# One fused attention, routing and two-MLP kernel: first transfers in a fixed order, another order inside attention, a shorter rational function, and all weight conversions behind the last routing

## The chip, the cores and the metric

One core of a Trainium2 chip runs the whole program in one launch. The metric is device time in microseconds (us). TensorE (PE) multiplies matrices, VectorE (DVE), ScalarE (ACT) and GpSimd (POOL) work on elements, SyncE (SP) issues nearly all transfers, in order.

## What is computed

```python
# 1: causal attention with decay; B, H, S, D = 4, 8, 576, 64
cum = cumsum(log(clip(f, 1e-4, 1)), -1)
scores = q @ k.T / sqrt(D) + cum[i] - cum[j]          # j <= i
x = softmax(scores) @ v                               # to 2304 tokens x 512
# 2: eight experts, one per token
logits = x @ w_gate + modality_bias[modality_id]
e, gate = argmax(logits), softmax(logits).max()
x = gate * (relu(x @ w1[e]) @ w2[e])                  # 512 -> 1024 -> 512
# 3: a second MLP with a rational activation
h = x @ w_in                                          # 512 -> 2048
g = (a0 + a1 h + a2 h^2 + a3 h^3) / (1 + |b0 h| + |b1| h^2 + 1e-6)
out = g @ w_out
```

`w_in`, `w_out`, `a` and `b` come as 64-bit floats; the rest is 32-bit.

## The kernel before

**Attention** works on 16 pairs of heads. For a pair, `load` brings k, q and v (nine transfers), `parts` turns k and q with PE and splits them into a high and a low part (`split`: a copy on ACT, a difference on DVE), `maxes` computes the scores once in four groups M0 to M3 to get each row's maximum (a DVE reduction per block), `turned` turns the maxima and sends them by two transfers into a row of the operand `qa`, `scores` computes the scores again in S0 to S3 with that row, exponentiates (ACT) and splits (ACT, POOL), and `values` multiplies with v in chunks (V) and divides. `logits` (L0, L1) of a finished pair turns its result and adds to the routing logits. The string `ORDER` writes down in which order PE takes these steps of four different pairs in one pass of the loop: M of pair p+1, S of p, V of p-1, L of p-2, T (`parts`) of p+2, m (`turned`) of p+1. While `nc.chained` is set, PE's steps keep their written order.

**Routing** (`Route`): after every fourth pair `batch` finds the expert of each of a batch's 576 tokens and scatters tokens to a table (five POOL transfers). After the last batch `final` plans the remaining work.

**Units**: 17 units multiply gathered tokens with one expert's `w1` and `w2`: two early single units of 128 tokens that can run before the last batch is routed, then eight doubles of 256 tokens, then seven singles. Each loads 16 pieces of 256 KB (tile `b`, four in flight) and splits each (ACT copy, DVE difference). A single has 48 matmuls of 512 columns; a double has 96 of 256 columns and 48 of 512. Their buffers take the place of attention's, so the first load waits for attention's end.

**Conversions** (`Weights.fill`, tag C): 32 blocks of 512 KB of `w_in` and `w_out` are loaded (two buffers), made into 32-bit floats by integer steps (ACT `Abs`, then on DVE one `tensor_scalar` and two `scalar_tensor_tensor`, tile `y`) and split (ACT, POOL). They need free memory: three blocks fit at once (`en`), the others take what attention gives back. The result is needed by all of the second MLP.

**Second MLP** (`Second.tile`): nine tiles of 256 tokens. Each has 8 steps of 24 matmuls of 256 columns into one bank, `rational` on it, and 12 matmuls of 512 columns. `rational` has, after ACT's `Ln` and `Exp` have given 1/Q, a Newton step on DVE, then the high part `gh` and the low part `gl`.

**What sets the order.** Every call is recorded in `Rec` and the program is put out by a planner (`flush`): each operation gets a cost, a key from the length of the work behind it plus a bonus (`nc.up`, `TB`), and list scheduling with modelled costs fixes each engine's and each queue's order. `Rec.order` holds pairs that fix the order of the plan alone: an engine still starts an instruction when its own inputs are there, and each engine keeps its order. Line 155 is the helper that all operations go through, so the profile shows `L155` for nearly all; `L713` is a grouped set of attention matmuls, `L1182` a unit's weight load.

## Time and profile before

| what | us |
|---|---|
| median of three runs (lowest, highest) | 1115.08 (1113.36, 1122.32) |
| the profiled execution's own time | 1123.07 |
| its span, first to last instruction | 1121.4 |
| busy in it: PE, DVE, ACT, POOL | 1003.1, 854.4, 651.3, 405.4 |

The profile is one execution, 1.67 us of which lie outside the span, and 8.0 us longer than the median. PE's busy time counts overlapping matmuls, so that it can be full while the matmuls come more slowly than they could.

### The profile page before, as it was taken

Reading aid. Unit: us, or ns where it says so; the run is one execution under the profiler, and the core shown is the slowest. Engines: PE = TensorE matmul, PEld = TensorE weight load, DVE = VectorE, ACT = ScalarE, POOL = GpSimd, SP = SyncE. Lnnn points to the kernel's source line nnn. Section 1 sums busy time; section 2 is a strip of 40 time slices with the busy share of each in tenths; the row PEclk is TensorE's granted clock in tenths of the full one; section 3 lists DMA queues with packets and bytes.
Section 4 is the critical chain, followed back from the end, with each engine's and each line's share of the span. In section 5 each row is a group of like instructions: output and inputs, shape, how many; then the busy total and the mean of one; then the engine's idle time right before and its main releaser. Section 6 shows DMA issues by size and latency. Waiting matters only on the chain.

```text
span 1121.4 us, 22693 instructions
## 1 busy us (share of the span) xinstructions
PE 1003.1 (89%) x8246; PEld 853.2 (76%) x8246; DVE 854.4 (76%) x1557; ACT 651.3 (58%) x1034; POOL 405.4 (36%) x353
## 2 busy tenths in 40 slices
PE   3689988898746799999999999999999999999995
PEld 2577777776634578879888898889878887888793
DVE  5775756758788896787869767949769969979685
ACT  1465554465545675656567466637658667676472
POOL 9576675676742431223122121212222223121131
PEclk9999998898758699999999999999999999999999
DMA  7663333211478887301151543445354454553400
GB/s 180 166 172 86 105 73 82 51 45 47 99 233 220 268 270 238 83 1 39 48 160 46 153 134 102 142 132 151 114 163 140 119 182 132 156 154 105 123 1 19
DMA packets 157376, 138.28 MB, mean 123 GB/s; under 512 B 73392, under 2 KB 115664, under 8 KB 157264
## 3 DMA queue, kind: packets, MB, share of 16 engines
q1 hardware_dynamic: 152288, 123.63, 39.1%
q0 software_dynamic: 4640, 13.13, 3.7%
q8 instruction: 64, 1.05, 0.4%
q14 instruction: 48, 0.39, 0.1%
q10 hardware_dynamic: 336, 0.08, 0.0%
HBM read 120.38 MB, written 16.33 MB: 122 GB/s over the span
## 4 chain that ended last, share of the span: by engine, by line
PE 50%; DVE 22%; DMA 9%; issue 9%; ACT 4%; POOL 2%; SPq 2%; DVEq 0%; POOLq 0%; ACTq 0%
PE pair L155 31%; PE one L155 13%; DVE y L155 12%; PE pair L713 6%; DMA b<-in_moe_w_dram 4%; DVE at L155 4%; DVE b L155 4%; ACT y L155 3%; DVE keep L155 2%; ACT b L155 1%; SPq L155 1%; DVE f32r L155 1%; POOL f32r L155 1%; POOL y L155 1%; DMA ys<-b 1%
## 5 line engine op out<-in xcount | busy, mean ns | idle before, releaser
L155 DVE TENSOR_TENSOR b<-b,b 128x512 fp32r<-128x512 f32 x272 | 200.5, 746 | 67.6 <-ACT b L155 36.4
L155 PE MATMUL pair<-b,b 128*128 128x256 f32 (+1 forms) x1032 | 234.8, 329 | 16.5 <-DVE b L155 10.2
L155 ACT CAST b<-b 128x512 fp32r<-128x512 f32 x272 | 165.1, 618 | 124.4 <-PE one L155 46.1
L155 POOL TENSOR_TENSOR y<-y,y 128x512 f32<-128x512 f32 x72 | 107.3, 1491 | 302.4 <-ACT y L155 284.0
L155 PEld LDWEIGHTS pair<-b,b 128*128 128x128 f32 x1032 | 174.1, 198 | 50.2 <-DVE b L155 19.0
L155 PE MATMUL one<-b,b 128*128 128x512 f32 x552 | 181.1, 404 | 5.1 <-DVE b L155 3.3
L713 PE MATMUL pair<-f32r 64*128 64x288 f32 (+4 forms) x1152 | 128.6, 343 | 16.5 <-ACT f32r L155 6.8
L155 ACT ACTIVATE y<-y,keep 128x512 f32<-128x512 f32 x144 | 109.3, 769 | 36.1 <-POOL y L155 29.1
L155 POOL TENSOR_TENSOR old<-old,at 128x960 f16<-128x960 f32 (+1 forms) x64 | 109.6, 1724 | 46.6 <-ACT at L155 46.3
L155 DVE SCALAR_TENSOR_TENSOR y<-y,keep,y 128x512 f32<-128x512 f32 x144 | 116.9, 822 | 7.9 <-ACT y L155 4.6
L713 PEld LDWEIGHTS pair<-f32r 64*128 64x128 f32 x1152 | 94.6, 204 | 25.3 <-ACT f32r L155 7.3
L155 PE MATMUL pair<-f32r,y 128*128 128x512 f32 x378 | 110.9, 397 | 1.7 <-DVE y L155 1.6
L155 PEld LDWEIGHTS one<-b,b 128*128 128x128 f32 x552 | 95.7, 188 | 21.9 <-DVE b L155 6.8
L155 PE MATMUL pair<-y,f32r 128*128 128x256 f32 x624 | 103.8, 283 | 1.8 <-DVE y L155 1.8
L155 PEld LDWEIGHTS pair<-y,f32r 128*128 128x128 f32 x624 | 91.7, 188 | 9.3 <-DVE y L155 3.4
L155 ACT ACTIVATE old<-pair,keep 128x960 f32<-128x960 f32 (+1 forms) x64 | 59.4, 928 | 66.9 <-PE pair L713 63.9
L155 DVE TENSOR_REDUCE at<-pair 128x2 f32<-128x576 f32 (+1 forms) x96 | 66.2, 707 | 34.8 <-PE pair L713 30.6
L155 PE MATMUL pair<-at,y 128*128 128x512 f32 x270 | 90.1, 410 | 1.7 <-DVE y L155 1.4
L155 ACT ACTIVATE y<-y 128x512 f32<-128x512 f32 x104 | 66.8, 643 | 31.0 <-DMA y<-in_moe_w_in_dram 23.9
L155 PEld LDWEIGHTS pair<-f32r,y 128*128 128x128 f32 x378 | 67.8, 188 | 16.2 <-DVE y L155 4.1
L155 POOL DMA_INDIRECT keep<-xnat,keep x32 | 34.4, 1075 | 120.3 <-PE pair L155 50.9
L155 ACT ACTIVATE y<-pair,keep 128x512 f32<-128x512 f32 x70 | 54.3, 776 | 25.0 <-DVE y L155 20.2
(140 smaller groups left out, 1872.9 us busy)
## 6 DMA issues: line engine op xcount, KB each, us to landing
b<-in_moe_w_dram SPq DMA_DIRECT2D x272, 256.0 KB
y<-in_moe_w_in_dram SPq DMA_DIRECT2D x16, 512.0 KB
y<-in_moe_w_out_dram SPq DMA_DIRECT2D x16, 512.0 KB
ys<-b SPq DMA_DIRECT2D x25, 257.0 KB
y<-ys SPq DMA_DIRECT2D x18, 257.0 KB
prep<-in_v_dram SPq DMA_DIRECT2D x4, 1152.0 KB
prep<-in_q_dram SPq DMA_DIRECT2D x32, 128.0 KB
prep<-in_v_dram SPq DMA_DIRECT2D x32, 128.0 KB
```

The source lines that it names most:

```text
L155: fn = lambda: getattr(getattr(s.nc, eng), name)(*(x() for x in ra), **{n: x() for n, x in rk.items()})
L713: T.matmul(o, lhsT=w, rhs=x, start=st, stop=sp, skip_group_check=True)
```

## The change

- **Prologue.** `prep` is cut into `load`, `loadv`, `sums` and `vparts`. With `nc.line` set, SP's transfers keep their written order: k and q of pairs 0 and 1, the gate weights, the decay sums, v of pair 0, both pairs' rows of sums, the large v load of `squares`, v of pair 1, the modality data, the zeroed table; then pair 2's. The decay sums are computed in other buffers, so that pair 0's load no longer waits for them. Pair 1's `parts` come ahead of pair 0's `maxes`, and `ro.setup`, `scales` and `vparts` are recorded after `turned`.
- **Attention's order.** M3 follows M2, T1 follows T0, L0 comes after V2, m0 after S2. M2's reductions are planned after the last reciprocal of `values`.
- **Rational.** The Newton step, the copy and its choice of engine go. `gh` is the product itself, rounded; `gl` comes from the remainder. One constant's sign changes.
- **Conversions.** All 32, their loads among them, are planned after the last operation of `ro.final()`.

```diff
+        if e == "D" and s.line:
+
+            if s.tail is not None:
+                s.order.append((s.tail, i))
+            s.tail = i
+        if s.gate is not None:
+            s.order.append((s.gate, i))
...
+    def squares(s, b):
...
+        s.nc.sync.dma_start(out=sv, in_=s.v[n:n + 8 * S].rearrange("(k p c) d -> p k (c d)", k=4, p=P))
...
         for b, j0, n, off in s.ROWS[g]:
+            if g == 2 and s.done is not None:
+
+                s.nc.order.append((s.done, len(s.nc.ops)))
...
                     V.reciprocal(r, r)
+                    s.done = len(s.nc.ops)
...
-        V.scalar_tensor_tensor(z, z, c["qc"], ab, op0=ALU.add, op1=ALU.mult)
-        V.scalar_tensor_tensor(z, z, -2.0, ab, op0=ALU.add, op1=ALU.mult)
-        V.scalar_tensor_tensor(u, u, c["na0"], z, op0=ALU.add, op1=ALU.mult)
+
         gh, gl = s.gh.next(), s.gl.next()
-        s.n += 1
-        if s.GH[s.n % len(s.GH)] == "A":
-            A.copy(gh, u)
-        else:
-            V.tensor_copy(gh, u)
-        V.tensor_sub(gl, u, gh.bitcast(F32))
+        V.scalar_tensor_tensor(gh, u, c["na0"], ab, op0=ALU.add, op1=ALU.mult)
+        V.scalar_tensor_tensor(z, z, c["qc"], gh.bitcast(F32), op0=ALU.add, op1=ALU.mult)
+        V.scalar_tensor_tensor(z, u, c["na0"], z, op0=ALU.add, op1=ALU.subtract)
+        V.tensor_tensor(gl, z, ab, op=ALU.mult)
...
-ORDER = "M0V5S0V6M1V7S1M2L0v0V1T0M3V2S2m0V3T1S3L1V4"
+ORDER = "M0V5S0V6M1V7S1M2M3v0V1T0T1V2L0S2m0V3S3L1V4"
...
+        nc.line = True
+        at.load(0)
+        at.load(1)
+        nc.tag = ''
+        ro = Route(nc, keep, ya, prep, at.pe.bufs[3].rearrange("p h n -> p (h n)"), banks, dr, moe_modality_id, moe_w_gate, moe_modality_bias, c)
         at.setup(f32r)
         late()
-        ro = Route(nc, keep, ya, prep, at.pe.bufs[1].rearrange("p h n -> p (h n)"), banks, dr, moe_modality_id, moe_w_gate, moe_modality_bias, c)
-        ro.setup()
+        at.loadv(0)
+        for p in range(2):
+            at.sums(p)
+        at.squares(0)
+        at.loadv(1)
+        ro.load()
+        nc.line, nc.tag = False, ''
         un = Units(nc, keep, dr, ro, moe_w1, moe_w2, c)
         wt = Weights(nc, ya, moe2_w_in, moe2_w_out)
-        nc.up = u["conv"]
-        wt.fill(en())
         nc.up = u["a"]
-        at.scales(0, ro.sw)
+        nc.chained = True
         for p in range(2):
-            at.prep(p)
-        nc.chained = True
-        for _ in at.parts(0):
-            pass
+            for _ in at.parts(p):
+                pass
         for g in range(4):
             at.maxes(0, g)
         at.turned(0)
-        for _ in at.parts(1):
-            pass
+        nc.tag = ''
+        ro.setup()
+        at.scales(0, ro.sw)
+        for p in range(2):
+            at.vparts(p)
...
             if p + 2 < NP:
+                nc.line = not p
                 at.prep(p + 2)
+                nc.line = False
...
-        nc.up = u["conv"]
-        wt.fill(pn())
-        wt.fill(fn())
         nc.up = u["route"]
         ro.batch(B - 1)
         ro.final()
+
+        nc.gate = len(nc.ops) - 1
+        nc.up = u["conv"]
+        wt.fill(en())
+        wt.fill(pn())
+        wt.fill(fn())
         nc.up = u["conv2"]
         wt.fill(an())
+        nc.gate = None
```

## Rows read from the trace of the kernel before

**Rows 1.** The page, part 2: busy tenths in 40 slices of 28 us.

```profile
PE   3689988898746799999999999999999999999995
...
DVE  5775756758788896787869767949769969979685
...
DMA  7663333211478887301151543445354454553400
```

**Rows 2.** Windows: length, then busy time of engines, PEclk, DMA share, GB/s.

```profile
300.00:350.00 50.00, 27.66 (x224) 21.06 (x221) 42.88 (x113) 23.78 (x41) 24.20 (x19) 0.69 0.77 203
350.00:400.00 50.00, 37.93 (x143) 26.00 (x143) 41.35 (x71) 30.01 (x53) 17.60 (x14) 0.80 0.83 256
```

**Rows 3.** The chain that ended last: start, length, what.

```profile
21.86 3.29 DMA f32r<-cums
...
33.65 4.70 DMA y<-in_moe_w_in_dram
...
305.19 5.05 DMA y<-in_moe_w_out_dram
312.02 6.05 DMA b<-in_moe_w_dram
```

**Rows 4.** Timeline, 0 to 45 us: start, length, instruction, idle time before.

```profile
10.46 0.74 DVE L155 TENSOR_TENSOR f32r<-prep,f32r 32x576 fp32r<-32x576 f32 x1
...
28.86 0.30 DVE L155 TENSOR_SCALAR keep<-keep 128x5 int32<-128x5 int32 x3 [3.54 <-POOL keep L155]
...
38.38 0.66 ACT L155 ACTIVATE y<-y 128x512 f32<-128x512 f32 x1 [18.96 <-DMA y<-in_moe_w_in_dram]
...
40.16 1.22 PE L713 MATMUL pair<-f32r 64*128 64x288 f32 x8 [4.13 <-ACT f32r L155]
```

**Rows 5.** SyncE's queue: transfers of the pairs' row maxima.

```profile
36.25 1.65 SPq L155 DMA_DIRECT2D f32r<-f32r  x2
...
81.77 1.51 SPq L155 DMA_DIRECT2D f32r<-f32r  x2
...
111.21 1.51 SPq L155 DMA_DIRECT2D f32r<-f32r  x2
...
260.06 1.42 SPq L155 DMA_DIRECT2D f32r<-f32r  x2
...
279.52 1.42 SPq L155 DMA_DIRECT2D f32r<-f32r  x2
```

**Rows 6.** Waits of PE, 75:145, then 250:300: total, times, longest.

```profile
PE pair L155 <- DVE y L155: 3.0, 5, 0.7
...
PE pair L155 <- DVE y L155: 5.2, 3, 3.9
```

**Rows 7.** Groups of instructions: count, busy us, mean ns, idle before.

```profile
L155 DVE TENSOR_TENSOR b<-b,b 128x512 fp32r<-128x512 f32 x272 | 200.5, 746 | 67.6 <-ACT b L155 36.4 <-PE pair L155 18.2 <-PE one L155 7.9
...
L155 DVE SCALAR_TENSOR_TENSOR y<-y,keep,y 128x512 f32<-128x512 f32 x144 | 116.9, 822 | 7.9 <-ACT y L155 4.6 <-POOL y L155 2.3
...
L155 DVE SCALAR_TENSOR_TENSOR y<-y,y 128x512 f32<-128x512 f32 x72 | 56.4, 783 | 0.6
...
L155 DVE SCALAR_TENSOR_TENSOR y<-y 128x512 int32<-128x512 int32 (+1 forms) x65 | 54.6, 842 | 0.9
...
L155 DVE CAST y<-y 128x512 fp32r<-128x512 f32 x72 | 40.2, 558 | 3.4 <-PE pair L155 2.9
...
L155 DVE TENSOR_SCALAR y<-y 128x512 int32<-128x512 int32 (+3 forms) x35 | 20.6, 588 | 5.9 <-ACT y L155 5.7
```

**Rows 8.** ACT's groups of instructions, 0 to 310 us: the conversions' `Abs` alone.

```profile
L155 ACT ACTIVATE y<-y 128x512 f32<-128x512 f32 x12 | 8.0, 669 | 21.8 <-DMA y<-in_moe_w_in_dram 21.8
```

**Rows 9.** Tile b (unit weights) in one window, columns as in rows 2.

```profile
310.00:455.00 145.00, 102.33 (x463) 76.19 (x463) 69.49 (x100) 61.01 (x104) 0.83 0.83 244
```

**Rows 10.** Timeline of PE, last tile: start, length, instruction, count.

```profile
1072.79 5.51 PE L155 MATMUL pair<-y,f32r 128*128 128x256 f32 x45
...
1079.41 3.88 PE L155 MATMUL pair<-prep,y 128*128 128x512 f32 x16
```

More of the change, by code (lines that the diff above doesn't have):

```diff
@@ L57, in __init__ @@
         s.chained, s.link = False, None
+        s.line, s.tail, s.gate = False, None, None
         for e in s.ENG:
@@ L570, in __init__ @@
         s.cums = dr.tile([2 * NP, 2, S], F32, name="cums")
-        s.T, s.A, s.Pm, s.x, s.vh, s.raws, s.sc, s.inv = {}, {}, {}, {}, {}, {}, {}, {}
+        s.done = None
+        s.T, s.A, s.Pm, s.x, s.vh, s.raws, s.sc, s.inv, s.svs, s.vrs = ({} for _ in range(10))
         for t in s.vr.bufs:
             V.memset(t[64:P, :, 4], 0.0)
-        s.ft = s.raw.bufs[0].rearrange("p a b c -> p (a b c)")[:32, :S]
+        s.ft, s.zz = (s.hi.bufs[1][:32, i, :2 * S].bitcast(F32) for i in range(2))
         nc.scalar.dma_start(out=s.ft, in_=f.rearrange("b h s -> (b h) s"))
@@ L624, in scales @@
         nc, c, V = s.nc, s.c, s.nc.vector
-        sv, n2, sc, iv = s.sv.next(), s.n2.next(), s.scr.next(), s.scr.next()
-        n = 8 * S * b
-        nc.sync.dma_start(out=sv, in_=s.v[n:n + 8 * S].rearrange("(k p c) d -> p k (c d)", k=4, p=P))
+        sv, n2, sc, iv = s.svs.pop(b), s.n2.next(), s.scr.next(), s.scr.next()
         pm = s.banks["x"].next()
@@ L644, in scales, with load @@
             s.sc[4 * b + k], s.inv[4 * b + k] = sc[:, k:k + 1], iv[:, k:k + 1]
-    def prep(s, p):
+    def load(s, p):
         s.nc.tag = f'P{p}'
-        nc = s.nc
-        raw, vr = s.raw.next(), s.vr.next()
-        a = 2 * S * p
+        nc, raw, a = s.nc, s.raw.next(), 2 * S * p
         for i, src in enumerate((s.k, s.q)):
@@ L655, in prep, with loadv @@
             nc.sync.dma_start(out=raw[:64, i, 4].rearrange("p (h d) -> p h d", h=2), in_=src[a:a + 2 * S].rearrange("(h p) d -> p h d", h=2)[512:])
+        s.raws[p] = raw
+    def loadv(s, p):
+        s.nc.tag = f'P{p}'
+        nc, vr, a = s.nc, s.vr.next(), 2 * S * p
         for h in range(2):
@@ L658, in prep, with sums, vparts @@
         nc.sync.dma_start(out=vr[:64, :, 4], in_=s.v[a:a + 2 * S].rearrange("(h p) d -> p h d", h=2)[512:])
-        s.raws[p] = raw
-        ka, qa = s.ka.next(), s.qa.next()
-        s.A[p] = ka, qa
+        s.vrs[p] = vr
+    def sums(s, p):
+        s.nc.tag = f'P{p}'
+        ka, qa = s.A[p] = s.ka.next(), s.qa.next()
         for h in range(2):
-            nc.sync.dma_start(out=ka[64 * h + 32:64 * h + 34, 64:64 + S].bitcast(F32), in_=s.cums[2 * p + h])
-        vb = s.vh[p] = s.vt.next()
+            s.nc.sync.dma_start(out=ka[64 * h + 32:64 * h + 34, 64:64 + S].bitcast(F32), in_=s.cums[2 * p + h])
+    def vparts(s, p):
+        s.nc.tag = f'P{p}'
+        vr, vb = s.vrs.pop(p), s.vt.next()
+        s.vh[p] = vb
         v, vt, f = vr.rearrange("p h b d -> p (h b) d"), vb.rearrange("p h b d -> p (h b) d"), s.sc[p]
-        G = nc.gpsimd
+        G = s.nc.gpsimd
         G.tensor_scalar(vt[:, :, D:2 * D], v, f, 0.0, op0=ALU.mult, op1=ALU.add)
@@ L669, in prep @@
         G.tensor_tensor(vt[:, :, :D], v, vt[:, :, D:2 * D], op=ALU.subtract)
+    def prep(s, p):
+        s.load(p)
+        s.loadv(p)
+        s.sums(p)
+        s.vparts(p)
     def parts(s, p):
@@ L833, in __init__, with load @@
         V.memset(s.md, 0)
-        md = s.md
-        nc.sync.dma_start(out=s.table.rearrange("(p c) t -> p (c t)", p=P), in_=z)
+        s.args = mod, mb, z
         nc.sync.dma_start(out=s.wg, in_=wg.rearrange("(k p) e -> p k e", p=P))
+    def load(s):
+        nc, md, (mod, mb, z) = s.nc, s.md, s.args
+        nc.tag = ''
         nc.sync.dma_start(out=s.bb, in_=mb.rearrange("(o m) e -> o m e", o=1).to_broadcast([P, 2, E]))
```

15 lines of the change are left out of this document (9 added, 6 removed).

## The prediction, made before the changed kernel ran

> **What bounds the kernel now.** I read the page's slices first. PE's row has its low digits in two places: the first slices (3, 6) and slices 11 to 14 (7, 4, 6, 7); from slice 15 on it reads 9 nearly throughout [rows 1]. The time is lost at the start and around 300 to 400 us; behind that PE is filled with matmuls, and only their density is left to gain. DMA has its highest digits (7, 8, 8 in slices 12 to 14) just where PE is low the second time, and 3 to 1 in attention before it [rows 1].
>
> The windows say what the second hole is. From 300 to 350 PE is busy for 27.66 of 50 us at a granted clock of 0.69 and DVE for 42.88; from 350 to 400 PE for 37.93 at 0.80, DVE for 41.35, with 256 GB/s moved at a DMA share of 0.83 [rows 2]. So DVE and the transfers are both near full while PE starves: unit weights, their splits and the conversions meet there. The chain that ended last passes through both holes and names conversions: it goes over the first rows of sums (issued at 21.86, landing 3.29 later at 25.15), over a load of w_in at 33.65, over one of w_out at 305.19 (5.05 us) and over a first weight load at 312.02 (6.05 us) [rows 3].
>
> How much the second hole holds: between 310 and 455 us the units have 463 matmuls [rows 9]. At full pace one of 512 columns takes 3.88/16, less the last one's overlap, about 0.2325 us, and one of 256 about 0.119 (5.51/45, likewise) [rows 10]. Two singles are 96 x 0.2325 = 22.3 us, a double 96 x 0.119 + 48 x 0.2325 = 22.6; the other 367 of the 463 are 367/144 = 2.55 doubles, 57.6 us. That is 80 us of work in 145: **65 us lost.**
>
> **The change part by part.** All sums are made against the profiled execution (1123.07 us, span 1121.4). It lies 8.0 above the median of the three runs; I take the same difference off the median.
>
> *Prologue.* The sums are ready on DVE at 10.46 + 0.74 = 11.2 us, and yet they land in the operand only at 25.15 [rows 3, 4]. With their write and read at the row's 3.29 each, and the first loads done early, they could be there at 11.2 + 2 x 3.29 = 17.8: 7.4 earlier. Thirteen transfers now stand ahead of the write on SP, and it is in turn ahead of v and the rows. POOL's fills of `ka` may end later than that, which the trace can't show; the gain is between 0 and 7.4, and I take 6. Next, DVE stood 3.54 us behind a POOL instruction of `ro.setup` before the reductions of the first maxima, and ACT stood until 38.38 for a load of a conversion while pair 1's split was queued behind it; PE idled 4.13 us for that split [rows 4]. The first goes as `setup` comes later, the second as no conversion is left there and pair 1 is turned first. Both delays ended at the same matmul at 40.16, so I count one: 3. What is late next is the transfer of the maxima. The scales, still needed by the first `values`, have a whole pass to hide in; were that cover gone, one pass of 14.7 us is the price. **Prologue: 9, bounds 0 to 13.**
>
> *Attention.* Sixteen transfers of maxima mark its pace: from 36.25 to 279.52 there are 15 periods, 243.3 us. Clean ones take (111.21 - 81.77)/2 = 14.72 [rows 5]; 15 of them would be 220.8. Of the 22.5 over, the last period has 19.46 - 14.72 = 4.7 and the first three together 45.52 - 44.16 = 1.4, both with conversions queued on DVE and ACT: 6 goes. The rest belongs to the routing of batches and stays. The new order takes L0's turns away from directly behind the division they wait for: that wait was 3.0 us in five passes [rows 6], at most 0.6 x 15 = 9. But m0 loses T1 as cover on its way to the next S0, some 0.3 us of PE; between -5 and 9 I take 5. After 279.52, PE's longest wait on DVE was 3.9 us, at a conversion's operations, and the chain has the 5.05 us of w_out [rows 3, 6]; of these 9 I take 6. **Attention: 17, bounds 1 to 24.** The units' first load comes earlier by these 26 us.
>
> *Conversions.* All 32 now follow the end of routing; before, 12 were begun by 310 us [rows 8] and 20 came after. The two early singles need 32 pieces of 256 KB, at 256 GB/s [rows 2] 1.024 us each: 32.8 us plus a first landing of 6.05, against 22.3 of matmuls and some 2 of turns: 15 lost, with few conversions beside them. A conversion is 2.05 us of transfer and, by the groups, 0.588 + 2 x 0.842 = 2.27 of DVE [rows 7]; a double is 16.4 of transfer and, with 16 splits of 0.746 and six evacuations taken at the same price, 16.4 of DVE. Either leaves 6.2 us beside a double's 22.6 of PE, so three conversions are free per double. Spread over all eight doubles, 131 + 72.7 of DVE stand against 181 of PE: 23 lost. Packed into 5.5 of them, 90 + 72.7 against 124: 39 lost. The planner fills idle queues early, so I take 34, nearer the packed end. The stage loses 15 + 34 = 49 in place of 65. **Conversions: 16, bounds -57 to 50** (the ends are priced with the rivals).
>
> The Trainium skill (DMA: Bandwidth & Descriptors, Specifications) gives a core some 358 GB/s of HBM. By that rule a double with 5.8 conversions, 7.2 MB, would take an estimated 20 us, under its 22.6 of PE; the 256 GB/s of the window from 350 us [rows 2] gives 28, and the trace of before has no fuller stretch among its rows.
>
> *Rational.* Two `scalar_tensor_tensor` with a third after them, a cast and a difference become three and a product: one of 0.783 and the cast of 0.558 go, one of 0.822 comes for the other old form kept [rows 7]. Counted whole, seven DVE operations become six: 0.783 + 0.822 + 0.822 + 0.558 before the difference against 3 x 0.822 before the product, 0.52 us less, 72 times: 37 us of DVE. `gh` is ready after one operation instead of four. DVE is not the bound everywhere: of the 24 slices from 449 us on, eight read 9 on DVE [rows 1], so a third, 12, would reach PE's pace; with the end of the last tile, where the chain from `Exp` shortens by 2.2 us, I take 10. Were DVE never the last, 2 is left; were it always, 37. **Rational: 10, bounds 2 to 37.**
>
> Sum: 9 + 17 + 16 + 10 = 52. 1123.07 - 52 = 1071; on the median 1115.08 - 52 = **1063**.
>
> **The rivals.**
>
> *Conversions hide almost wholly* (chance 0.20). The planner spreads them, or DMA has the room that a share of 0.83 leaves (256/0.83 = 308 GB/s). Then the stage loses 15 to 31 and gains 42: 9 + 17 + 42 + 10 = 78, 1037 us. For it: DMA falls to 0 and 1 in slices 18 to 20 [rows 1], so there is room later. Against it: before, the plan did not use that room, and DVE's 72.7 us don't depend on transfers.
>
> *What is gained before is given back there* (0.13). The conversions' DVE work isn't hidden at all, and the clock stays low while PE waits: 15 + 72.7, and 16 more for 80 us of work at a clock of 0.83 [rows 9]: 104 lost, -39. Then 36 - 39: 1118, no change.
>
> *The conversions become a serial chain* (0.09). Two load buffers mean 16 rounds; at the chain's 5.05 for a landing and 0.66 for the `Abs` [rows 3, 4] these are 91 us, all exposed if the second MLP is what PE waits for. 15 + 91 + 16 = 122, -57: 1136, slower. It decides from some 112 us lost in the stage on, which eats all other gains and 11 more. For it: attention's idle transfers (3 to 1 in rows 1) are no longer used for any conversion. Against it: eight doubles give PE other work meanwhile.
>
> The Trainium skill (Perfetto Trace Analysis, Optimization Strategy) says that regimes bound by different engines may gain by being interleaved. The change moves 12 of 32 conversions out of a stage with idle transfers into one that is full of them, which by that rule is this rival.
>
> *The fixed order does not do what it says* (0.05). SP stands at `loadv` of pair 2, whose buffer pair 0's `vparts` must free on POOL, and holds up the maxima behind it. One lost pass of 14.7 and no gain at the start: 1063 + 9 + 5, with the rest as forecast 1077.
>
> **How the numbers follow.** The forecast as summed has 0.53, its own range 1045 to 1085. Measured differences under 1% (11 us) can't be told from none. Faster by over 1%: 0.53 + 0.20 + 0.05 = 0.78; within 1%: 0.13; slower: 0.09. For 8 in 10 the range goes down past the first rival (1037, with rational's or attention's upper part some 9 more), to 1028, and up to 1108, short of the second rival's middle and the third.
>
> **What would show it.** Right: first rows of sums landed near 19 us, the second pair's maxima some 9 earlier; last maxima transfer about 250 to 262; first weight load at 283 to 290; no conversion load before that; the two early singles done within 40 us of it; 72 fewer casts and 0.5 us less DVE per rational. The step on conversions is wrong if PE loses less than 35 or more than 60 us between the first weight load and the last conversion, or if PE's waits there name transfers of weights for most of it; the step on rational if DVE still reads 9 in the late slices; the step on attention if clean periods are not within 14.2 to 14.8.

## The result, and the profile after

The changed kernel takes 1102.44 us (median of 3 runs, 1099.04 to 1105.2), the kernel before 1115.08: a ratio of 0.985 [0.981, 0.989]. It is faster by 12.6 us, where 52 were forecast. In the profiled executions the span falls from 1121.4 to 1100.7 us, by 20.7; since a kernel's profiled execution can lie 8 us beside its median (before: 1123.07 and 1115.08) and up to 10 (e17 below: 1104.90 and 1095.14), accounts made from profiles are good to no better than that.

The page's slices of the changed kernel, part 2, to be read beside [rows 1]:

```profile
PE   3899999997667888999999999999999999999995
...
DVE  6566768673769988877877778667759879889674
...
DMA  6544343202867888882010010334254454553300
```

The hole at the start is smaller, attention has its nines from slice 3 on, and the second hole has moved forward: it is in slices 10 to 16 (7, 6, 6, 7, 8, 8, 8) in place of 11 to 14, and longer. DMA's eights now reach to slice 18; slices 19 to 25 read 2, 0, 1, 0, 0, 1, 0, before 1, 1, 5, 1, 5, 4, 3.

The SyncE queue shows where the time was gained, and where the next trouble begins (start, length, what; the maxima first, then the units' first loads):

```profile
28.36 1.59 SPq L163 DMA_DIRECT2D f32r<-f32r  x2
...
46.48 1.53 SPq L163 DMA_DIRECT2D f32r<-f32r  x2
...
232.91 1.41 SPq L163 DMA_DIRECT2D f32r<-f32r  x2
...
246.37 1.40 SPq L163 DMA_DIRECT2D f32r<-f32r  x2
...
270.55 1.92 SPq L1219 DMA_DIRECT2D b<-in_moe_w_dram  x4
272.57 1.00 SPq L163 DMA_DIRECT2D xnat<-y  x2
276.22 16.30 SPq L1219 DMA_DIRECT2D b<-in_moe_w_dram  x11
293.37 0.35 SPq L163 DMA_DIRECT2D y<-in_moe_w_in_dram  x1
...
304.75 0.36 SPq L1345 DMA_DIRECT2D ys<-b  x1
311.59 0.34 SPq L1236 DMA_DIRECT2D keep<-table  x1
```

The first maxima go 7.9 us earlier than in [rows 5], the last 33.2 earlier (246.37 against 279.52), the first weight load 39.6 earlier (270.55; before it was issued at 310.1). So ahead of the units 39.6 us are won, where 26 were forecast. But 20.7 are left at the end: 18.9 are given back behind the first weight load. The last three rows are part of how. The first conversion is loaded at 293.37; the first single's rows are stored at 304.75; then SP issues nothing for 6.5 us, until the table fetch of the first double can go.

The same windows as [rows 2], and the units' own matmuls (tile b) over the two early singles and over the five doubles behind them:

```profile
300.00:350.00 50.00, 34.01 (x119) 23.40 (x120) 37.68 (x53) 27.99 (x50) 15.87 (x13) 0.76 0.75 243
350.00:400.00 50.00, 44.06 (x254) 35.48 (x252) 47.00 (x70) 33.19 (x59) 18.29 (x13) 1.00 0.83 262
...
270.00:341.00 71.00, 42.33 (x123) 26.00 (x124) 30.17 (x44) 27.70 (x48) 0.78 0.74 222
341.00:494.00 153.00, 132.09 (x757) 108.02 (x756) 86.45 (x125) 71.98 (x125) 0.98 0.85 266
```

The third row is the surprise: 71 us for two singles. Transfers there move 222 GB/s, less than the 266 in the row below it. The chain that ended last passes through this stretch on transfers (start, length, what):

```profile
259.93 4.92 DMA table<-keep
264.85 0.27 issue
265.11 2.53 DMA table<-keep
...
281.67 5.42 DMA b<-in_moe_w_dram
...
296.21 10.24 DMA b<-in_moe_w_dram
...
314.95 6.13 DMA b<-in_moe_w_dram
```

Attention's end now hangs on scatters of the routing (`table<-keep`), the singles on single weight loads; one of them takes 10.24 us to land, just behind the first conversions' loads.

**An account of PE.** All 8246 matmuls are in both traces, and counted by shape at the price of one behind another (0.232 us for 512 columns, 0.117 for 256, the others likewise) they are 887.7 us of work in every kernel here. (With the prediction's 0.119 for 256, every row's losses would be 5 us lower in sum, and their differences the same.) What a stretch lasts beyond its work is lost. Three stretches, us lost in each: up to the first weight load; from there until 560.6 us of work are left, where the changed kernel ends its fifth double; and the rest. Beside them the singles (first weight load to the second single's store), and when the last conversion was loaded and the first tile's rows went out:

```
                               span   first   singles | lost:   stage  rest | last    tile 0
                                      load            | before              | conv.   out
before                        1121.4  310.1    78.8   | 131.4   63.3   38.9 | 413.6   507.1
after                         1100.7  270.5    70.5   |  91.9   74.7   46.4 | 468.0   553.5
e1  after, old rational       1113.5  276.4    72.7   |  97.7   73.0   55.1 | 477.0   561.6
e2  after, old conversions    1108.5  293.5    73.9   | 114.7   61.6   44.4 | 403.5   490.3
e3  before, new rational      1125.9  312.7    71.6   | 133.9   64.5   39.8 | 424.5   506.2
e4  before, new conversions   1120.9  287.9    66.1   | 109.1   69.0   55.0 | 504.6   582.4
e5  before, new order         1115.0  300.2    71.5   | 121.5   65.2   40.6 | 410.2   501.7
e6  before, new prologue      1110.8  299.1    74.8   | 120.4   64.4   38.4 | 412.9   512.6
e7  six load buffers          1089.8  268.7    63.1   |  90.0   61.7   50.4 | 472.0   546.5
e8  gate behind singles       1099.5  267.4    59.7   |  88.8   65.2   57.9 | 497.7   579.0
e9  later fetch               1117.1  275.7    66.5   |  97.1   80.0   52.3 | 474.1   553.9
e10 e7 and e9                 1098.5  268.2    70.2   |  89.6   74.8   46.5 | 467.5   543.6
e12 no conversions            1081.4  279.0    57.2   | 100.2   46.1   47.3 |   -     423.8
e14 singles among tiles       1130.5  278.7    72.6   | 100.1   75.8   66.9 | 476.2   634.5
e15 e7 and e14                1100.3  270.0    65.2   |  91.4   65.6   55.7 | 477.3   616.8
e16 e7 and e8                 1100.2  271.1    56.0   |  92.5   56.6   63.4 | 486.0   568.4
e17 e7, e8 and e9             1102.8  276.5    52.1   |  97.7   58.4   59.0 | 495.9   573.1
e18 e7, gate at attention     1091.6  266.9    74.9   |  88.3   67.5   48.1 | 445.4   530.6
```

After against before: -39.5, +11.4, +7.5. The forecast had -26, -16 and -10. The experiments are about the last two.

Each row is one execution. The thirteen kernels that have the changed attention with no conversion beside it (e13 among them, with 273.8) have their first weight load between 266.9 and 279.0 us, so a difference of some 10 us in one column proves little alone; where the intervals of the times don't overlap, a difference is shown.

**The clock in the account.** All work is priced at full pace, so "lost" also holds what the granted clock took. A wait of PE in the changed kernel's singles, and the window behind it:

```profile
302.08 1.92 PE L163 MATMUL pair<-b,b 128*128 128x512 f32 x3 [3.12 <-ACT b L163]
```

```profile
301.40:311.60 10.20, 7.69 (x15) 4.31 (x15) 7.62 (x11) 5.80 (x10) 2.68 (x3) 0.50 0.48 173
```

The granted clock is 0.50 there, the lower of its two levels (1.2 GHz), and 15 matmuls keep PE busy for 7.69 us; at 0.232 they are 3.5. Of the 70.5 us of the singles 30.8 had the lower level, where matmuls of 512 columns follow each other at 0.427 us. By the account's prices 13.0 us of work began in these parts, so an estimate of what the clock cost is 13.0 x (0.427/0.232 - 1) = 11 of the 41.8 us that the singles lose. For another 23.4 PE is idle. The same estimate gives 14 us for the singles of before, 7 in e12 and 4 in e17.

### The profile page after: what moved, and what is told of

It is laid out like the page before. It is cut to its first block, busy times and chain, and to the rows that moved or that the text cites. A ratio compares the mean times of both kernels' runs of the same rounds, so it can differ in the third digit from the quotient of the medians.

```text
span 1100.7 us, 22578 instructions
## 1 busy us (share of the span) xinstructions
PE 994.6 (90%) x8246; PEld 845.9 (77%) x8246; DVE 824.7 (75%) x1484; ACT 656.6 (60%) x1034; POOL 393.3 (36%) x353
## 4 chain that ended last, share of the span: by engine, by line
PE 53%; DVE 19%; DMA 13%; issue 5%; ACT 5%; POOL 2%; SPq 1%; POOLq 0%; DVEq 0%; ACTq 0%
PE pair L163 36%; PE one L163 11%; DVE y L163 10%; PE pair L742 6%; DMA b<-in_moe_w_dram 6%; DVE b L163 5%; ACT y L163 3%; DVE keep L163 2%; DVE at L163 2%; DMA table<-keep 2%; DMA prep<-in_v_dram 1%; ACT b L163 1%; POOL old L163 1%; DMA ys<-b 1%; DMA y<-in_moe_w_out_dram 1%
## 5 line engine op out<-in xcount | busy, mean ns | idle before, releaser
L163 PE MATMUL pair<-b,b 128*128 128x256 f32 (+1 forms) x1032 | 220.1, 330 | 27.4 <-ACT b L163 13.3
L163 POOL TENSOR_TENSOR y<-y,y 128x512 f32<-128x512 f32 x72 | 99.4, 1380 | 316.2 <-ACT y L163 296.4
L163 PEld LDWEIGHTS pair<-b,b 128*128 128x128 f32 x1032 | 165.0, 199 | 57.8 <-DVE b L163 20.4
L163 DVE SCALAR_TENSOR_TENSOR y<-y,keep,y 128x512 f32<-128x512 f32 (+1 forms) x216 | 177.9, 832 | 19.4 <-ACT y L163 11.9
L163 PE MATMUL one<-b,b 128*128 128x512 f32 x552 | 175.4, 407 | 13.0 <-ACT b L163 8.1
L742 PE MATMUL pair<-f32r 64*128 64x288 f32 (+4 forms) x1152 | 123.7, 334 | 12.0 <-DVE at L163 7.0
L163 PEld LDWEIGHTS one<-b,b 128*128 128x128 f32 x552 | 94.5, 189 | 35.0 <-DVE b L163 12.8
L163 PE MATMUL pair<-f32r,y 128*128 128x512 f32 x378 | 104.7, 398 | 0.0
L163 ACT ACTIVATE old<-pair,keep 128x960 f32<-128x960 f32 (+1 forms) x64 | 59.2, 925 | 70.4 <-PE pair L742 63.4
L163 DVE TENSOR_REDUCE at<-pair 128x2 f32<-128x576 f32 (+2 forms) x96 | 65.3, 707 | 34.7 <-PE pair L742 29.3
L163 PE MATMUL pair<-at,y 128*128 128x512 f32 x270 | 79.8, 406 | 5.5 <-DVE y L163 5.5
L163 ACT ACTIVATE y<-y 128x512 f32<-128x512 f32 x104 | 66.9, 644 | 22.1 <-DMA y<-in_moe_w_in_dram 12.5
L163 DVE TENSOR_TENSOR y<-y,pair 128x512 f32<-128x512 f32 x70 | 47.7, 682 | 28.0 <-ACT y L163 27.6
```

What stands on the lines that cost most here:

```text
L163: fn = lambda: getattr(getattr(s.nc, eng), name)(*(x() for x in ra), **{n: x() for n, x in rk.items()})
L742: T.matmul(o, lhsT=w, rhs=x, start=st, stop=sp, skip_group_check=True)
```

## The experiments

**One part taken back.** e1 is the changed kernel with the Newton step, the copy and the difference of before.

```diff
-        V.scalar_tensor_tensor(gh, u, c["na0"], ab, op0=ALU.add, op1=ALU.mult)
...
+        V.scalar_tensor_tensor(z, z, -2.0, ab, op0=ALU.add, op1=ALU.mult)
...
+            V.tensor_copy(gh, u)
+        V.tensor_sub(gl, u, gh.bitcast(F32))
```

> The changed kernel with the old rational function (Newton step and copy) put back. The forecast's term says the new one is worth 10 us, so this should take about 1112 us. The rival theory says that DVE is not what the late stages wait for, since PE waited on tile y for only 9 us behind 500 us in the changed kernel and for 4 before: then it stays within 3 us of the changed kernel's 1102.

Measured: 0.993 [0.990, 0.996], 0.8% above the changed kernel. The intervals don't overlap, so the new form is worth something here. Its span is 12.8 longer, but 5.9 of that lie ahead of the first weight load, where no rational is computed. Behind it the two profiles differ by 6.9 us: 8.7 in the rest (55.1 against 46.4), less 1.7 in the stage.

e2 is the changed kernel with the conversions where they were.

```diff
+        nc.up = u["conv"]
+        wt.fill(en())
...
-        nc.gate = len(nc.ops) - 1
```

> The changed kernel with the conversions recorded where they were before: three blocks in the prologue, the others ahead of the last batch's routing, no gate. If moving them is what gave the start's gain back (theory A: 12 more conversions in the stage that is already full of transfers, at 2.05 us each), this is faster than the changed kernel by 8 to 20 us: 1082 to 1094. If the early units are slow by their own loads (theory B: four buffers, a landing of 5 to 6 us each) and the place of the conversions is neutral, it stays at 1098 to 1107. By the forecast it would be slower, about 1118 or more.

Measured: 0.997 [0.993, 1.001], a median of 1117.48. That is the forecast's answer (slower than the changed kernel, about 1118), and neither theory's. Without the conversions' new place almost nothing is left of the gain: the first weight load comes at 293.5, the stage loses 61.6 in place of 74.7. So by the profiles the new place wins 23 us ahead of the units and costs 15 behind the first load (13 of them in the stage). This run's profiled execution lies 7.3 below its median; by the times the place is worth 1.2%, more than these 8 us.

**One part alone**, in the kernel before: e3 the rational, e4 the conversions, e5 the order, e6 the prologue; each diff is its part of the whole change; e4's:

```diff
+        nc.gate = len(nc.ops) - 1
+        nc.up = u["conv"]
+        wt.fill(en())
```

> The kernel before with the new rational function alone. Forecast: 10 us less, 1105. If DVE is not what the late stages wait for: 1112 to 1117, with some 37 us less of DVE busy time all the same.

> The kernel before with all conversions behind the last routing, and nothing else changed. Forecast: 16 us in the stage plus some 9 us of stalls that conversions cause earlier: about 1090. Theory A: the stalls go (9 us) and the stage gives back 12 x 2.05 = 25 us: about 1130. Theory B: 1106, the stalls alone.

> The kernel before with attention's new order alone (and the reductions planned behind the last reciprocal). The forecast's step gives it 5 us: 0.995 of before. A rival reading of the two traces: the eleven middle periods between transfers of maxima fell from 16.2 to 14.6 us, and 14.7 where the old conversions are put back, so the order is worth 1.2 to 1.5 a period, 13 to 16 us by the last transfer of maxima: that one near 264 us, and 0.987. If only the whole conversion stage absorbs what comes earlier, the first weight load is earlier by 13 or more and the end by less than 8.

> The kernel before with the new prologue alone: old order, old rational function, old place of the conversions. Forecast: 9 us, 0.992. Rival (the fixed order holds up the passes behind it): the first transfer of maxima comes 4 to 8 us earlier, but nothing of it is left by the third pair, and the time is 0.998 to 1.002.

Measured, in this order: 1.004 [1.000, 1.007], 1.005 [1.002, 1.007], 0.997 [0.994, 1.000], 1.000 [0.997, 1.003]. No part alone is faster by 1%; taken one after another they would make half a per cent slower, and together they are 1.5% faster. The account shows what each does. The rational is worth nothing there; that its operations ran beside work that was the bound is likely, but not shown. The order brings the first weight load 9.9 us forward, the prologue 11.0; either is within the scatter of single profiles, but with the conversions' 22.2 they make 43, near the 39.6 of all together. The conversions lose 5.7 more in the stage and 16.1 more in the rest, so nothing of their 22.2 is left. What wins most in attention, and what loses it later, is the same step.

**Why the singles are slow.** A load of a unit's weights is issued right when the split of the piece four before ends (276.22, 277.78, 278.57 us and the eight behind them, each 0.03 behind one), for there are four load buffers. e7 gives six, and two of each split's in place of three.

```diff
-RW = (4, 3, 3)
+RW = (6, 2, 2)
```

> The changed kernel with six load buffers for unit weights and two each for their high and low parts, in place of four, three and three: the same memory. In the changed kernel a weight load is issued right when the low part of the piece four before it is done, and the two early singles take 70 us. If these four buffers and the landing set that pace (theory of the ring), the early singles take 55 to 62 us and the total falls by 5 to 12, 1090 to 1097 or 0.975 to 0.98 of before. If transfers themselves are full there (forecast's step), nothing changes, or it is slower since PE has only two weight tiles: 0.985 or more.

Measured: 0.982 [0.979, 0.986]; singles 63.1 in place of 70.5, and 11 us less span. The interval overlaps the changed kernel's, so a gain in time isn't shown. All of the 7.4 us lie in the second single: the first takes 34.3 us, as it did with four (34.2). e8 keeps the ring and holds the conversions back until both singles are recorded.

```diff
+        early = len(nc.ops) - 1
...
-        nc.gate = len(nc.ops) - 1
+        nc.gate = early
```

> The changed kernel with the conversions planned behind the end of the second early unit and not behind the routing, so that no conversion runs beside the early singles. If conversions beside them make them slow (70 us where 39 were forecast), they now take 50 to 55 us, and the doubles' part grows by at most 8: 1090 to 1097. If their own loads and the routing's chain do, they stay at 64 to 70 us, the conversions end later, and the time is 1100 to 1110.

Measured: 0.986 [0.981, 0.990]; singles 59.7, and no gain in time: the stage loses 9.5 less, the rest 11.5 more (2.2 of both is one wait that falls on the boundary between them).

e9 plans the first double's table fetch, for which SP stands still from 305 to 311 us, behind the last load of the second single.

```diff
+                    if j == EARLY:
+                        nc.order += [(un.lastload, x) for x in range(n0, len(nc.ops)) if nc.ops[x][0] in "SD"]
```

> The changed kernel; in the planner's order the table fetch of the first double is put behind the last weight load of the second early single, where in the changed kernel it stands on SP from 304.75 to 311.59 us, waiting for the last scatter of the routing, with weight loads queued behind it. Theory (the early singles, 70.5 us from the first weight load to the second store, are slowed by their transfers: the ring of load buffers, this stall and the conversions): the stall goes, the two singles take about 63 us, and the time is 4 to 7 us less, ratio to the kernel before about 0.980. Rival A (the loads behind the stall were not what PE waited for): singles 68 to 71 us, time unchanged, 0.983 to 0.988. Rival B (the later fetch delays the first double by what the singles gain): singles about 63, the first double's store no earlier against the first weight load than 100 us as now, time unchanged.

> The changed kernel with six load buffers in place of four (two of each split kept in place of three) and the later table fetch together. Theory: the two causes are separate, so their gains add: singles about 56 us (70.5 less 7 for the buffers, less 7 for the stall), ratio to the kernel before 0.974 to 0.980. Rival (the time saved in the singles is taken back by the doubles beside the same conversions, as it was when the gate of the conversions was moved): singles 56 us, but the ratio stays at 0.982 to 0.986 and the stretch from the first weight load to the end stays above 820 us.

Measured: 0.994 [0.991, 0.998] and 0.985 [0.978, 0.993]. The singles of e9 take 66.5, but the first double is stored 37.5 us behind them (in the changed kernel 30), and the whole is slower: worse than either rival. In e10 the singles take 70.2: the conversions began at 285.3 there, 8 us earlier, and may have filled the room; that is not shown.

**What the conversions cost.**

```diff
-            nc.sync.dma_start(out=t.rearrange("p n t -> p (n t)"), in_=src)
...
+            nc.gpsimd.memset(h.bitcast(F32), 0.03)
+            nc.gpsimd.memset(l.bitcast(F32), 0.0)
```

> The changed kernel with the 32 conversions of the second MLP's weights left out (their loads, integer steps and splits); the weights are filled by POOL with constants, so this part of the work is missing. It measures what the conversions cost behind the last routing. The forecast's step: 34 us in the doubles, so about 1068 us, ratio 0.955. Theory (the doubles lose what was forecast, and the conversions beside the second early single cost about 10 more): 40 to 50 us, ratio 0.94 to 0.95, and the two singles take 55 to 62 us. Rival A (DVE's and ACT's work for them is not hidden at all, the second rival of the forecast): 65 us or more, ratio below 0.93. Rival B (they are all but hidden and the loss lies with the units' own transfers): less than 15 us, ratio above 0.97, and the doubles still take 30 us each.

Measured: 0.964 [0.957, 0.972]. Behind the first weight load 93.4 us are lost in place of 121.1, so the conversions cost 28 there: 11 in the singles (30.8 lost in place of 41.8) and 17 later, less than the theory's 40 to 50 and near the forecast's 34. They are mostly hidden; but the singles lose 30.8 without any. The 11 us aren't the conversions' alone: e12's plan also puts the last routing later, its first scatter at 299.5 us in place of 280.6, and of the 11 some 4 are the clock's by the estimate above.

e13 gives that kernel ten load buffers.

> The kernel without conversions (this part of the work is missing, the weights are constants), and the space of their load buffers given to the units' weights: ten load buffers in place of four. Without the ten buffers the two early singles took 57.2 us and PE lost 30.8 of them. Theory (a load is issued only when the piece four before it has been split, some 1.5 us a piece instead of 1.02): singles about 45 us, PE's loss in them near 18, and the time from the first weight load to the end some 10 less than 802. Rival A (SP waits for the scatters of the last batch before it issues the next loads): the loads of the first single come early, but a gap in the issue of some 5 to 12 us stays behind the last scatter and the singles take 52 to 57. Rival B (the transfers themselves are the pace, with 16 engines near full): issue to landing grows to 10 us or more and the singles stay at 55 or more.

The SyncE queue of this run:

```profile
273.78 1.91 SPq L1220 DMA_DIRECT2D b<-in_moe_w_dram  x4
275.94 1.67 SPq L1220 DMA_DIRECT2D y<-in_moe_w_dram  x3
...
298.59 0.36 SPq L1346 DMA_DIRECT2D ys<-b  x1
310.20 0.87 SPq L1237 DMA_DIRECT2D keep<-table  x2
311.32 1.49 SPq L1220 DMA_DIRECT2D b<-in_moe_w_dram  x3
```

and the last scatter of the routing on POOL, with the idle time before it:

```profile
307.29 0.91 POOL L163 DMA_INDIRECT table<-keep  x1 [2.92 <-DMA table<-keep]
```

The first single is stored 24.8 us after its first load (34.2 in the changed kernel). That this is the ring isn't shown: e12, with four buffers, needs 25.5, though with the last routing out of its way, and e7, with six and the conversions, 34.3. The first single of e12:

```profile
278.98 1.98 SPq L1211 DMA_DIRECT2D b<-in_moe_w_dram  x4
...
304.48 0.36 SPq L1337 DMA_DIRECT2D ys<-b  x1
```

Over both singles ten buffers gain nothing without conversions (58.6 us against 57.2, where 45 was expected), so the theory isn't borne out. Rival A's gap is seen: SP is silent for 11.3 us until the table fetch, which goes 2.9 us behind the last scatter, and the next weight loads stand behind it. But PE's longest wait in the singles names neither weights nor their splits:

```profile
319.14 1.12 PE L163 MATMUL pair<-keep 128*128 128x128 f32 x4 [11.28 <-DMA keep<-xnat,keep]
```

PE turns the gathered tokens of the first double here, in the middle of the second single. They are fetched by that table, and PE takes its matmuls in the order of the plan, so it stood for 11.28 us. The five doubles behind them, with no conversion beside, take 137.7 us, and PE loses 17.5 of these, 3.5 a double. The run's time (1142.88, one run) is no argument on the conversions: its first tile's rows go out only at 715 us (423.8 in e12), probably because the added buffers hold memory that the tiles need, and all nine run alone.

**The tiles.** e14 lets tile 1's matmuls go behind the first late single, tile 2's behind the second, and so on; e15 adds the six buffers.

```diff
+            if 0 < T <= NS:
+                nc.order += [(ends[ND + T - 1], x) for x in range(n0, len(nc.ops)) if nc.ops[x][0] == "T"]
```

> The changed kernel; in the planner's order the matmuls of tile 1 of the second MLP come behind the first late single, those of tile 2 behind the second, and so on; all up to the end of the doubles is the same. Theory (tiles alone leave PE some 7 us a tile in turns that a unit's matmuls would fill; the kernel before had units among its tiles from the start and lost 7.5 us where the changed kernel loses 12.1): the loss behind the doubles falls from 46.4 to about 38, the time by 6 to 9 us, ratio 0.977 to 0.980. Rival A (the singles' loads and splits on DVE get in the tiles' way by as much): unchanged, 0.983 to 0.988. Rival B (the tiles at the end are then alone in place of those in the middle): the loss moves from 494 to 700 us to behind 850, total unchanged.

> The changed kernel with six load buffers (ratio 0.9822 by themselves) and the late singles among the tiles. Theory: both gains add, ratio 0.973 to 0.977 and about 1087 us. Rival: the singles among the tiles bring nothing, 0.980 to 0.984.

Measured: 1.002 [0.999, 1.006] and 0.981 [0.976, 0.986]. The theory falls in this form: the rest loses 66.9, not 38. From 629 to 1016 us, where tiles and singles take turns, 34.4 of 387 us are lost (8.9%), and the changed kernel lost 32.0 of 544 between 501 and 1045.

**Taking the singles' troubles away together.**

> The changed kernel with six load buffers, and the conversions held until the early singles are recorded. Theory (ring and conversions slow the singles apart from each other, 7 and 11 us): singles about 52 us with PE losing some 24 in them; the conversions then lie beside the doubles alone, which take 156 us or more; ratio 0.980 to 0.985, no better than the six buffers alone (0.9822). Rival (what the singles gain is kept): 0.972 to 0.976.

> The same with the first double's table fetch behind the last load of the second single. Theory (three causes: ring, conversions, the fetch on SP): singles 45 to 48 us; the first double then comes late, as it did with the later fetch alone (38 us for it in place of 30), so that the ratio is 0.982 to 0.990. Rival (the fetch was the larger part): singles 45 and ratio below 0.978.

Measured: 0.984 [0.982, 0.987] and 0.981 [0.978, 0.984]. The singles now take 56.0 and 52.1, 14 and 18 us less than in the changed kernel, and the end doesn't come earlier than with six buffers alone: the loss of the rest is 63.4 and 59.0, with six buffers alone 50.4. The windows of e16 show where it went:

```profile
300.00:340.00 40.00, 33.90 (x163) 26.26 (x164) 24.39 (x38) 23.64 (x41) 6.23 (x6) 0.87 0.88 259
...
500.00:550.00 50.00, 43.02 (x288) 40.08 (x287) 33.31 (x48) 25.49 (x42) 8.43 (x6) 0.93 0.26 78
```

and of the changed kernel:

```profile
300.00:340.00 40.00, 26.18 (x73) 16.12 (x74) 29.77 (x43) 22.25 (x40) 13.01 (x11) 0.74 0.72 239
...
500.00:550.00 50.00, 49.62 (x319) 44.44 (x320) 39.18 (x55) 29.50 (x45) 12.04 (x9) 1.00 0.08 26
```

In the singles e16 has 163 matmuls for 73. From 500 to 550, where the changed kernel is in its first tile with PE busy for 49.62 us, e16 has 43.02: its last conversion was loaded at 486.0, 18 later, and its first tile is 15 later. That is the pattern of the table's last columns: where no order holds the tiles back, the first tile's rows go out 74 to 86 us behind the load of the last conversion if the conversions are gated (82 to 100 if not), and that load comes 158 to 182 us behind the first one. Whether the singles are quick or slow, the second MLP begins when the gated conversions are through. That its begin sets the end of the kernel is argued from this pattern, and two rows go against it: e12 has its first tile at 423.8 and e2 at 490.3, and their rest loses 47.3 and 44.4, about what it loses where the first tile comes near 545 (e7 50.4, e10 46.5).

**The gate itself.** If so, an earlier gate must bring the first tile forward though it hurts the singles. e18 has the six buffers and the gate at attention's end.

```diff
+        early = len(nc.ops) - 1
         while i < EARLY:
...
-        nc.gate = len(nc.ops) - 1
+        nc.gate = early
```

> The changed kernel with six load buffers (0.9822 by themselves, first tile out at 546.5) and the gate of the conversions at the end of attention, ahead of the last routing and the early singles. Theory (the gate and the 160 to 180 us of transfers behind it set when the second MLP starts): conversions from about 268, the last one at 445 to 455 in place of 472, the first tile's rows out at 525 to 533, PE's loss in the singles up again to 40 or more, and the time 5 to 12 us less than with the six buffers alone, ratio 0.971 to 0.978. Rival (the transfers of units and conversions together are the limit, whoever comes first): the last conversion at 465 to 472 again as with the later fetch, where it began at 285, and the ratio 0.981 to 0.985.

Measured: 0.974 [0.970, 0.978], 1089.7 us. The last conversion's load and the first tile's rows in this run:

```profile
445.43 0.48 SPq L163 DMA_DIRECT2D y<-in_moe_w_out_dram  x1
```

```profile
530.62 0.99 POOL L163 DMA_INDIRECT out_dram<-y,keep  x1 [3.28 <-DMA out_dram<-y,keep]
```

The same two in the changed kernel:

```profile
468.03 0.37 SPq L163 DMA_DIRECT2D y<-in_moe_w_out_dram  x1
```

```profile
553.52 0.98 POOL L163 DMA_INDIRECT out_dram<-y,keep  x1 [3.41 <-DMA out_dram<-y,keep]
```

Its windows:

```profile
300.00:340.00 40.00, 28.73 (x93) 17.79 (x91) 34.95 (x51) 24.94 (x44) 14.55 (x11) 0.87 0.86 272
340.00:400.00 60.00, 56.06 (x341) 46.69 (x341) 55.95 (x85) 42.66 (x75) 19.77 (x15) 1.00 0.94 290
...
460.00:500.00 40.00, 39.25 (x262) 35.01 (x261) 27.36 (x44) 24.09 (x41) 7.46 (x6) 1.00 0.50 152
```

All marks of the theory are met: conversions from 267.9 to 445.4, the first tile out at 530.6 (forecast 525 to 533), the singles up to 74.9 with 46.2 lost, and yet the fastest of the complete kernels. It beats the kernel before by 2.6% and lies below the changed kernel's ratio with no overlap of the intervals; the six buffers alone had 0.982 [0.979, 0.986], which it clears by a hair. The profiles don't show where the time was won: e18's is its slowest execution (1093.28, median 1089.70), e7's its fastest (1091.50, median 1095.56), and by the account e18 loses 5.8 us more in the stage than e7 and 2.3 less in the rest.

## Why the prediction was wrong

**Prologue, 9: about right alone, by another way.** The rows of sums were written at 11.91 and read at 15.27, and the first scores went on at 17.19, earlier than the mark of 19. The trace has no landing for these reads, and names a fill on POOL as what PE waited for last; the forecast had named such fills. The first maxima came 7.9 earlier. But the second came only 3.9 earlier, not 9 (46.48, before 50.4): the gain at the start was half given back in the second pass. By e6 the part moved the first weight load 11 us forward, and the time not at all (1.000).

**Attention, 17: too small.** Together with the prologue 39.6 us instead of 26. The mean period of the maxima is now (246.37 - 28.36)/15 = 14.53, within the mark of 14.2 to 14.8; it was 243.3/15 = 16.2. The step took 14.72 from two periods of [rows 5] as the clean pace, counted 6.1 of the 22.5 over it as conversions', and let the rest stay as the routing's. More than all of it went, 25.3 (243.3 - 218.0): by e4 the conversions' leaving alone is worth 22 us, and the order, by e5, 10 where 5 was taken. The stalls were sized by named waits; what the conversions cost in passes without one was left out. This error went the other way from the next one and hid part of it: without these 13.6 us more than forecast ahead of the units the time would lie near 1116, outside the wide range (1028 to 1108) too. That it lies inside is luck.

**Conversions, 16 gained: the step that failed.** It had the stage lose 49 in place of 65. By the account it loses 74.7; before, the same work lost 63.3, so the 65 from which the step started was near. Its two terms:

- *The early singles, 15.* They lost 41.8: 70.5 us, where 39 was the mark. The term had their pace from 256 GB/s and one landing, which needs loads that are always under way. They were not: with four buffers a load goes only when a split ends, SP stands 6.5 us for a scatter of the last routing, and the first conversion is loaded at 293.37, in the first single. Taken away one at a time, the singles get 7.4 us shorter by six buffers (e7), 4.0 by the later fetch (e9) and 10.8 by later conversions (e8), and 18.4 by all three (e17). The term also took the 22.3 us of matmuls at full pace, though [rows 2] had a granted clock of 0.69 at this place; the lower clock cost some 11, by the estimate above.
- *The doubles, 34.* They lost 32.9, 152.5 us for five. The number was right and its cause only in part: a double by itself loses 3.5 (e13), which makes 17.5, and what e12 lays to the conversions behind the singles is 17.

Beneath both terms lies the larger error. The step added up losses of PE, as if a shorter part would end the stage sooner. e8, e16 and e17 made the singles up to 18 us shorter, and the rest lost most of it again. What the first tile waits for is the chain from the gate over the 32 conversions, and the change has put its end from 413.6 to 468.0 us, and the first tile from 507.1 to 553.5, while the first weight load came 39.6 earlier. The two in the kernel before:

```profile
413.56 0.35 SPq L155 DMA_DIRECT2D y<-in_moe_w_out_dram  x1
```

```profile
507.14 1.34 POOL L155 DMA_INDIRECT out_dram<-y,keep  x1 [2.55 <-ACT b L155]
```

e18 supports that this start matters for the time; how much of the miss is its, and how much the singles' and the clock's, the runs don't separate. By the prediction's own sign the step was wrong: some 71 us were lost between the first weight load and the last conversion, where 35 to 60 were allowed. The third rival had this chain in sight, but as two buffers' rounds of 91 us; it took 175, paced by transfers that it shares with the units (266 GB/s at a share of 0.85), and most of it beside useful work.

The Trainium skill (Perfetto Trace Analysis, Optimization Strategy) says that regimes bound by different engines may gain by being interleaved. The runs here agree in one place: with six buffers and the conversions begun 29 us earlier (267.9 against 297.0), over the last routing and the singles, the ratio falls from 0.982 to 0.974. In the other place they don't: laid back into attention, whose transfers have room (a share of 0.39 from 100 to 200 us, 0.15 to 265), the conversions make the changed kernel slower (e2, 0.997 in place of 0.985).

**Rational, 10: about right in the changed kernel, nothing in the kernel before.** 72 casts went; DVE is busy for 824.7 us, before 854.4, 30 less in all. The rational's own operations of 128x512 fall from 270.4 us (three groups of [rows 7] and the difference, shown first) to 234.5, which is 35.9 of the 37 counted:

```profile
L155 DVE TENSOR_TENSOR y<-y,y 128x512 fp32r<-128x512 f32 x72 | 56.9, 790 | 2.9 <-PE pair L155 1.6
```

and in the changed kernel:

```profile
L163 DVE SCALAR_TENSOR_TENSOR y<-y,keep,y 128x512 f32<-128x512 f32 x144 | 117.8, 820 | 5.6 <-DVE y L163 0.5
L163 DVE SCALAR_TENSOR_TENSOR y<-y,keep,y 128x512 fp32r<-128x512 f32 x72 | 61.6, 855 | 13.8 <-ACT y L163 11.9 <-PE pair L163 1.8
L163 DVE TENSOR_TENSOR y<-y,y 128x512 fp32r<-128x512 f32 x72 | 55.1, 766 | 3.3 <-PE pair L163 1.3
```

The three operations cost (117.8 + 61.6)/72 = 2.49 us a time, and the product 0.77. By e1 the form is worth 0.8% (6.9 us behind the first weight load in the profiles), by e3 nothing. DVE still reads 9 in three of the late slices, before in eight. But the forecast counted these 10 on a late part that otherwise stays, and that part now loses 7.5 more. By e4 the conversions' place costs 16.1 there: before, the first tile was out at 507, with e4's change at 582.4.

**The second rival** (1118, no change) is the one the outcome resembles, and its main term isn't what happened: the conversions cost 28 us in all by e12, so most of their 72.7 us of DVE work is hidden. Its other term, the clock (16 us), was there, with some 11, but the kernel before had it too, with some 14. The fourth rival's lost pass didn't occur (the second maxima follow the first after 18.1 us, 3.6 above the mean period); its price is added up wrong, since a lost pass of 14.7 and the 9 of the prologue make 1087 and not 1077.

**What stays open.** Why the parts, 0.5% slower one by one, make 1.5% together: by e2 and e4 the conversions' place costs 15 us after the first load in the new kernel and 22 in the old, and that is seen but not explained. And a part of the singles' loss (30.2 us with ten buffers and no conversions) was not taken apart further than PE's wait of 11.28 and, as an estimate like the one above, 5 of the clock.

## What to carry to other kernels

When work is moved behind a point, ask first what can't start until it is done, and write the time of that start down for both orders; losses of the bound engine in the stretch between come second, and mending them need not end the stage sooner. A pace taken from bandwidth holds only with loads always under way: look at what releases a load's issue, and at what stands ahead of it in its queue. An earlier start of such a chain can pay though it slows its neighbours (e18), but idle transfers alone don't make a good place for it (e2): look at what its other engines are doing there. A sum of matmuls at full pace lacks a term where the trace of before shows a low granted clock.

## What was unexpected of the hardware

- A chain of scatters to one table has a long pace: the last five in the changed kernel were issued at 280.6, 284.8, 292.2, 297.7 and 306.5 us, the last four with POOL idle for 3.2 to 7.9 us until the one before had landed, and the fetch behind them blocked SP's whole queue.
- The weight loads of 256 KB on the chain that ended last took 3.6 to 6.8 us to land in the changed kernel (ten of them), and 10.24 the one that was issued at 296.2, behind conversions' loads of 512 KB at 293.37 and 294.35.
- The transfers can go faster than the 256 GB/s on which the forecast rested: 290 GB/s over 60 us in e18, at a share of 0.94.
- Attention in the same order took 270.5 us to the first weight load in one execution (the changed kernel) and 278.7 in another (e14). From 100 to 200 us the granted clock was 0.97 in the first, with 1601 matmuls, and 0.92 in the second, with 1464. A few us in one stretch of a single profile decide nothing.
- Tiles alone lost 12% of the time (37.3 of 308 us in e13), units alone 13% (17.5 of 138); mixed as in the kernel before, from 455 to 1050 us, 4.5% (26.9 of 595), but mixed as in e14 8.9%.
